# Attention layer with a gated MLP: first half's down projection as Strassen products of tile pairs, and sums divided between VectorE and GpSimd by a table

## The chip, the cores and the metric

The kernel runs on one core of one Trainium2 chip. The metric is the device time of one execution in microseconds (us), the median of several runs; smaller is better. TensorE multiplies 128x128 weights with up to 512 columns into PSUM, VectorE and GpSimd do element-wise work and reductions, ScalarE does activations and copies, and SyncE (SP) issues most of the DMAs. In the profile they are PE, DVE, POOL, ACT and SP.

## The reference, cut to what matters

One layer on 2048 tokens of width 512, in fp32: the normalized input goes through a linear attention of 32 heads of width 16 and, beside it, through a gated MLP with 1376 hidden units; the attention's output is scaled by silu of the MLP's output and added to the input.

```python
x  = A_x
xn = _layernorm(x, axis=-1)
s  = _A_ref(xn, A_wqkv, A_w_phi, A_wo)
g  = _silu(_B_ref(xn, B_W_gate, B_W_up, B_W_down))
return x + s * g
# _A_ref: phi_q, phi_k = [softmax(+q W_phi), softmax(-q W_phi)] per head, the same of k
#         kv = phi_k^T v ;  z = sum of phi_k ;  o = (phi_q kv) / (phi_q z + 1e-6) ;  o @ wo
# _B_ref: gate = xn @ W_gate ;  up = xn @ W_up ;  h = where(gate > 0, gate, 0) * up
#         return h @ W_down
```

## The kernel before, in words

**Numbers.** Each fp32 operand of a product is split into a high and a low part. ScalarE copies the value into the high part, rounded, and a subtraction on another engine leaves the low part. A product of fp32 quality is then three matmuls (low x high, high x low, high x high), `mm3` at L233. So each matrix that enters a product costs one ScalarE copy and one subtraction, and the subtraction is one of the "sums" that this text speaks of.

**Tiles and halves.** Tokens stand in 16 row tiles of 128; a half of the program's MLP work has 8 of them, seen as two blocks of 512 columns (`BT`). The 1376 hidden units stand in NF = 11 tiles of 128; the last, KEPT = 10, has no partner. The blocks of the normalized, transposed input (`XT`) are combined by Strassen's scheme: `GATE_BLOCKS` are seven combinations, for two blocks of tokens against two halves of the width.

**First half's gate and up projection** (`gate_ops`, L845). For hidden tile f, steps `g{f}.0` to `g{f}.6` are seven Strassen products of 6 matmuls each (2 k-tiles x 3), into three PSUM banks (`ga`, `gc`, `gd`) and a fixed bank `seed`. ScalarE copies `ga` out, then VectorE makes five sums and two fused relu-times-up operations, each with at least one operand in PSUM. The results, `h` of two blocks, are split into `hh` pairs.

**First half's down projection** (`down_ops` L888, `down_part` L893, `last_rows` L1082, all through `down_rows`). For chunks of two hidden tiles (`CHUNKS`, the last has three), and each of the 8 row tiles, 3 matmuls per hidden tile accumulate in a bank `py`, with `hh` as the weight and the split down weights `fd` as the moving matrix. Per chunk and row tile one operation folds the bank onto the output `Y0`/`Y1` in SBUF: ScalarE for the first chunk, VectorE for the others. There are 264 such matmuls, 8 ScalarE copies and 32 VectorE folds. The down weights are loaded, ordered and split by `prep_ops` (L413, `fd<-rawd`), and stored to DRAM (`putfe`) for later use beside the gate weights.

**Second half.** The gate (`gate_ops_2`, L1169) uses two banks and hands `seed` to ScalarE three times per tile, so that VectorE has two sums and two fused operations. The down projection takes hidden tiles by pairs: `PAIRED` has five. For a pair, `pair_weight_ops` (L1257) loads two raw tiles of down weights (`WR`), makes four sums of them (`TT`), and splits the matrices `DA`, `DB`, `DC`, `DD`; `pair_hidden_ops` (L1310) makes four sums of the hidden tiles (`S1` to `S4`) and splits seven matrices into `hh` pairs; `pair_down_ops` (L1327) multiplies them, seven Strassen products of 3 matmuls for each of two column halves, in banks `pA`, `pU`, `pD`, each folded by VectorE onto a transposed output `YT0`/`YT1`. The single tile 10 goes by `single_down_ops` (L1229, bank `pE`). At the end `turn_back_ops` (L1367) applies silu, transposes 32x32 blocks on VectorE, and writes the result to DRAM (`YD`), from which it is loaded as rows (`yd`).

**Attention.** 16 key tiles (`key_ops` L670, `kv_ops`) come before the state; 8 queries' worth of pairs (`query_half_ops`, L932) come after it; `QUERIES` says which are turned by halves, through PSUM, and which whole. The output tiles (`out_tile_ops`, L1118) multiply by `wo` (bank `pso`), then multiply with y and add the input: `yd<-pso,yd` on VectorE, `yd<-yd,sx` on GpSimd, in the last row tile on VectorE.

**What sets the order.** Nothing is scheduled by the compiler: `Plan` (L153) holds a closure per operation name, and `Plan.run` calls them in the order of a written table, `ORDER` (L56 to L150), 2075 names before and 2190 after. `InOrder` (L172) keeps that order on each engine. That is why every instruction in the profile has one line, L184 (in the changed kernel L204). A second table, `PLACES` (L43), gives each buffer its place: two-, four- and eight-KB buffers in SBUF (`u2`, `u4`, `u8`) and seven PSUM banks (`ps`). An instruction waits for its operands, and for the last reader of the buffer that it overwrites.

**Which engine sums.** Before, each call of `add` (L222) names its engine. Sums with an operand in PSUM are on VectorE; nearly all sums of two SBUF operands (low parts, Strassen sums of weights and hidden tiles, `yd<-yd,sx`) are on GpSimd.

Of the kernel before, what the change touches and what calls it, by code (L numbers as in the profile page):

```python
# [16 lines left out]
H = 32  # L17
# [12 lines left out]
QUERIES = [(0, 1, 2), (3, 4, 5, 6, 7)]  # L30
BY_VECTOR, IDLE = 4, 8
KEPT = NF - 1
PAIRED = [(2 * p, 2 * p + 1) for p in range(NF // 2)]
WO_WITH = (4, 5, 6, 7)
# [5 lines left out]
0101011010010101001001  # L40

0123456789abcdefghijklmn7kh2a9kng287ldhkg8dgkhgdkh8kdh8kghd10d89a43k2nl7cb1ji08hcg65fe304jh1lbdankjm
9bl53ef07nj2bdf4jhml2b6c1i0kd4bk8em16g5aed213hjc0e4fln5c0h5ci1ebj29gm0iel1348fkb2154jaigdb24f87k36mc  # L43
5l179da304625m9c1he3adjbifnlh7362b8nfljh3a1ig2j6h1lf0knmb2ejn148hf3kigb489fnhag051c78eb50difnagj75lc
h06i275be8gmh5a4f9lcmh63f1ead4kmh17cj94kgfilbd2hnm34i9g0c

0172345689abcd02453869ba5dc802a639bc57d42a576bc8d79c567ab84b56ad827a09b14c9a82c730281c54b9a467b94206
ac2318d52b3017a534c19024c6153ba241ac509c41bac7210a4cb5974c96174ba150689c348190dcb35a2863bc5249387954
86127ad69b

0123456013162504654236541306105302646411441616114646641441116161641646415302615416540412034601245621
4524062451346461425034256250325616162316540624354535415312301353025163240532160434163410653261463152
0635613504664256152601342450210305324612034265316151064125132360650635103665065421340
# [3 lines left out]
ld1 lk0 lcb Fk0 bn1 pw1 bi1 ap1 ld0 bn0 pw0 ap0 T1 kh0 lk1 Fk1 kl0 kh1 kl1 kc0 lk3 Fk3 lq0 hi1 lo1 T0 hi0 lo0 kc1  # L57
Fq1 lk2 Fk2 kh2 ld2 bn2 pw2 Fq0 pk0.0 pk0.1 kl2 pk0.2 kh3 kl3 pk0.3 bi2 qh0 ql0 qh1 ql1 sums0 lv0 pk1.0 pk1.1 pk1.2
pk1.3 vh_0 ld5 st5 td1 vh_1 vl_0 ld3 ep5 bn3 mx0 th1.0 tl1.0 th1.1 ap2 kc2 kc3 lq1 Fq2 pw3 bi3 T2 qh2 ql2 Fq3 pv0.0
lv1 vl_1 pv0.1 ap3 sh0 vh_2 hi2 lo2 T3 qh3 ql3 pw5 bi5 hi3 lo3 vl_2 vh_3 pv1.0 sums1 tl1.1 pv1.1 pv1.2 ld4 st4 ep4  # L60
vl_3 pw4 q1.1 ex0 sm0 td3 ld6 st6 ep6 pw6 sc0 mx1 ap5 pv1.3 vh1 ld7 st7 z0 ep7 pw7 spill0 ph0 bi4 ap4 pl0 sh1 ex1
vl1 td2 td4 pq1.1 q2.0 sps0 bi6 pk2.0 bi7 ap7 sps1 sm1 sc1 z1 pq2.0 pv0.2 pk2.1 pv0.3 vh0 pk2.2 T5 ld8 hi5 st8 T4
sums2 ap6 pv3.0 ep8 lo5 pw8 pv3.1 pv2.0 pv2.1 vl0 hi4 lo4 pv3.2 hS2 slo2 pk2.3 ld9 mx2 T7 T6 hi7 lo7 sh2 ph1 pv3.3
# [12 lines left out]
ql0.0 sums7 P7.6 P3.6 cW6 P4.6 hS7 slo7 lo15 lo14 P1.7 mx13 sh13 cS7 q6.1 pq6.1 sq6.1 fs0 ft0 fs1 ft1 ex13 mx12 sh12
P6.7 rw2 cU7 fa1 fal1 sm13 sc13 z13 sq4.1 ex12 sm12 P3.7 mx14 rd0 fc0 q6.0 kv10 fb0 fbl0 ph13 pl13 pq6.0 P7.7 fc1
sc12 rw4 P5.6 fs2 ft2 fcl0 aw6 z12 cW7 P4.7 P5.7 P2.6 ph12 pl12 sh14 rw3 aw7 sq6.0 P2.7 ex14 ql0.1 vh13 vl13 au6
sm14 au7 vh14 vl14 q8.0 putwc0 pq8.0 sq8.0 mx15 sh15 sc14 ex15 z14 fd1 fdl1 putwd1 fa0 fal0 putwb0 rd1 putwa0 q7.0
sm15 sc15 fe0 fel0 pq7.0 sq7.0 vh15 vl15 q8.1 pq8.1 rw5 kv13 vh12 kz vl12 sq8.1 qt0.0 ph15 pl15 qm0.0 qs0.0 q7.1  # L80
ql2.0 pq7.1 sq7.1 g0.0 z15 putwa1 g0.1 gt0 g0.2 g0.3 fa4 gm0 kv15 ge0 gf0 fb2 fb1 qe0.0 fs3 g0.4 gp0 qa0.0 gs0 fa2
g0.5 fbl1 fc2 fbl2 putwb2 fa3 ph14 kv12 pl14 ql1.0 fd4 fdl4 fal2 putwa2 of_1 g0.6 gn0 g1.1 qt0.1 gg0 qm0.1 fcl1
putwc1 putwd0 g1.0 gt1 sq3.1 kv14 fal3 fcl2 putwc2 ka kb ha0 g1.5 putwa3 ft3 hc0 hd0 zh zl of_2 fd2 g1.2 fdl2 g1.3
fc3 fcl3 hb0 putwc3 g3.0 gt3 qt2.0 gm1 ge1 gf1 g1.4 qs0.1 g1.6 kT g2.0 gp1 gs1 fe1 fel1 gn1 g2.1 fb3 fbl3 ha1 hb1
fal4 gg1 qt1.0 qm1.0 qs1.0 fd3 putwb1 fdl3 gt2 zp0 zc0 gm2 qe0.1 zp1 zc1 qw0.1 fs4 g2.2 putwd2 rw6 g2.5 g2.3 ge2 gf2
ql2.1 g2.4 gp2 kr gs2 ha2 ft4 fb4 putwd4 dn012 qw0.0 g3.1 hc1 qm2.0 qs2.0 kh1_ putwb3 rd3 fe3 fel3 putwa4 qe2.0
qb0.1 g2.6 g3.2 fbl4 gm3 dn010 hd1 rd5 sf1 dy010 sg1 sl1 ge3 g3.3 gf3 gn2 gg2 g3.4 fs5 ft5 putfe1 putfe0 qb0.0 gp3
# [65 lines left out]
class Plan:  # L153
# [8 lines left out]
    def run(self, order):  # L162
        last = {t: name for name in order for t in self.ops[name][1]}
        for name in order:
            fn, tiles = self.ops[name]
            fn()
            for t in tiles:
                if last[t] == name:
                    self.tiles.pop(t, None)
# [19 lines left out]
def layer_kernel(ctx: ExitStack, tc: tile.TileContext, x, wkT, wqT, wv, wo, wf, cst, out):  # L189
# [698 lines left out]
    def down_ops(c):  # L888
        for j in (1, 0):
            for i in range(TPB):  # L890
                down_part(c, j, i)
# [616 lines left out]
```

## Time and profile before

| | before |
|---|---|
| median of 3 runs | 550.25 us (550.11 to 551.11) |
| the profiled execution | 550.4 us |
| its span in the profile | 548.2 us |
| TensorE | 542.0 us busy, 2572 matmuls |
| VectorE | 440.0 us busy, 650 instructions |
| ScalarE | 310.3 us busy, 552 instructions |
| GpSimd | 468.7 us busy, 377 instructions |
| DMA | 132.99 MB, mean 243 GB/s |

The span is the time from the first to the last instruction that the hardware profiler records; the 2.2 us by which the execution is longer lie around it. A row of the view by groups reads: line, engine, operation, out<-in by the program's names, partitions x elements, count, then busy time and the mean of one in ns, then the idle time before them and what ended it. Busy shares are averages over the span; a wait counts only where the engine that waits is the one that sets the end.

### The profile page before, as it was taken

To read this page: it belongs to the slowest core of one execution; us is meant where nothing else is said; L and a number is where in the kernel's file an instruction comes from. 1 tells how busy PE (TensorE), PEld (TensorE's weight loads), DVE (VectorE), ACT (ScalarE), POOL (GpSimd) and SP (SyncE) were. 2 spreads that over 40 slices of the span, in tenths; PEclk is the share of its full clock that TensorE was granted. 3 is DMA by queue.
4 is the path that set the end of the run, shared out by engine and by line. 5 is a ranking of instruction groups with operands and counts; after the bars stand their busy time and mean duration, and the time that the engine had idled before them with its cause. 6 is when DMAs were issued, how large, how long until landed. Compare 5 with 4: busy or idle time off the path is not lost.

```text
span 548.2 us, 8110 instructions
## 1 busy us (share of the span) xinstructions
PE 542.0 (99%) x2572; PEld 454.4 (83%) x2572; DVE 440.0 (80%) x650; ACT 310.3 (57%) x552; POOL 468.7 (86%) x377
## 2 busy tenths in 40 slices
PE   8999999999999999999999999999999999999996
PEld 8888888888888888888888888888888888888885
DVE  5999898878857898998888636877799999984753
ACT  4998787776464457535353345547636555545620
POOL 1999668899999998998978867988989899999965
PEclk9999999999999999999999999999999999999999
DMA  8567737367898796898867899876755859789987
GB/s 305 210 192 239 192 78 192 77 158 211 228 315 273 283 308 213 259 347 291 281 227 275 248 266 375 342 249 215 242 179 180 288 162 266 226 277 293 240 236 265
DMA packets 83034, 132.99 MB, mean 243 GB/s; under 512 B 7344, under 2 KB 38448, under 8 KB 82096
## 3 DMA queue, kind: packets, MB, share of 16 engines
q1 hardware_dynamic: 79392, 119.83, 65.2%
q0 software_dynamic: 3456, 12.58, 12.0%
q8 instruction: 20, 0.33, 0.2%
q14 instruction: 22, 0.18, 0.1%
q10 hardware_dynamic: 144, 0.07, 0.0%
HBM read 70.58 MB, written 53.48 MB: 226 GB/s over the span
## 4 chain that ended last, share of the span: by engine, by line
PE 99%; DVE 0%; issue 0%
PE seed L184 16%; PE py L184 11%; PE pq L184 8%; PE pso L184 8%; PE gc L184 6%; PE gd L184 5%; PE GD L184 5%; PE ga L184 5%; PE GA L184 5%; PE pU L184 4%; PE pa L184 3%; PE pd L184 3%; PE pnum L184 3%; PE pkv L184 3%; PE pD L184 2%; PE pA L184 2%
## 5 line engine op out<-in xcount | busy, mean ns | idle before, releaser
L184 PE MATMUL py<-fd,hh 128*128 128x512 f32 x264 | 63.5, 389 | 0.0
L184 PEld LDWEIGHTS py<-fd,hh 128*128 128x128 f32 x264 | 49.4, 188 | 10.3
L184 POOL TENSOR_TENSOR phl<-ek,phl 128x1024 fp32r<-128x1024 f32 x16 | 40.2, 2514 | 5.2 <-ACT phl L184 5.1
L184 POOL TENSOR_TENSOR ez<-eq,zB 128x1024 f32<-128x1024 f32 x16 | 38.6, 2417 | 4.2 <-ACT eq L184 3.2
L184 PE MATMUL pso<-wo,oh 128*128 128x512 f32 (+1 forms) x136 | 39.8, 376 | 0.0
L184 DVE TENSOR_TENSOR y<-py,y 128x512 f32<-128x512 f32 x32 | 21.7, 683 | 16.2 <-PE py L184 16.1
L184 PE MATMUL ga<-XT,wa 128*128 128x512 f32 x132 | 33.6, 390 | 0.0
L184 PE MATMUL seed<-XT,WB 128*128 128x512 f32 x120 | 30.6, 390 | 0.0
L184 PE MATMUL GA<-XT,WA 128*128 128x512 f32 x120 | 30.6, 390 | 0.0
L184 ACT ACTIVATE eq<-pnum 128x512 f32<-128x512 f32 x32 | 18.6, 594 | 19.8 <-PE pnum L184 19.7
L184 PEld LDWEIGHTS pso<-wo,oh 128*128 128x128 f32 x136 | 25.0, 188 | 4.7
L184 PEld LDWEIGHTS ga<-XT,wa 128*128 128x128 f32 x132 | 24.6, 188 | 5.0
L184 POOL TENSOR_TENSOR pTl<-ez,pTh 128x1024 fp32r<-128x1024 f32 x10 | 24.3, 2432 | 3.4 <-ACT pTh L184 3.0
L184 PEld LDWEIGHTS GA<-XT,WA 128*128 128x128 f32 x120 | 22.3, 188 | 4.5
L184 PEld LDWEIGHTS seed<-XT,WB 128*128 128x128 f32 x120 | 22.2, 188 | 4.5
L184 PE MATMUL pso<-wo,ol 128*128 128x512 f32 (+1 forms) x68 | 25.6, 376 | 0.0
L184 POOL TENSOR_TENSOR ol<-of,oh 128x1024 fp32r<-128x1024 f32 x8 | 20.0, 2494 | 5.3 <-ACT oh L184 5.2
L184 ACT ACTIVATE eq<-eq 128x512 f32<-128x512 f32 x32 | 18.4, 624 | 8.2 <-DVE eq L184 8.2
L184 POOL DMA_DIRECT2D zacc<-ek x16 | 14.4, 899 | 8.2 <-PE seed L184 5.0
L184 POOL TENSOR_TENSOR lr<-lr,mhalf 128x1 f32<-128x1 f32 x16 | 9.4, 590 | 13.8 <-DVE lr L184 13.7
L184 DVE TENSOR_REDUCE sm<-ek 128x64 f32<-128x1024 f32 x16 | 19.4, 1212 | 2.2 <-ACT ek L184 2.0
L184 POOL TENSOR_TENSOR hh<-s,hh 128x512 fp32r<-128x512 f32 x15 | 20.2, 1371 | 0.9 <-DVE YT L184 0.9
(284 smaller groups left out, 1846.3 us busy)
## 6 DMA issues: line engine op xcount, KB each, us to landing
zacc<-ek POOLq DMA_DIRECT2D x16, 512.0 KB, 4.9
XT<-xts SPq DMA_DIRECT2D x7, 1024.0 KB, 8.8
rawg<-wf SPq DMA_DIRECT2D x11, 512.0 KB, 4.8
ws<-wc SPq DMA_DIRECT2D x20, 256.0 KB, 6.3
ws<-wb SPq DMA_DIRECT2D x20, 256.0 KB, 5.5
ws<-wa SPq DMA_DIRECT2D x20, 256.0 KB, 5.0
ws<-fd SPq DMA_DIRECT2D x20, 256.0 KB, 5.5
WA<-ws SPq DMA_DIRECT2D x20, 256.0 KB, 2.9
```

The costliest lines, as they stand in the source:

```text
L184: return self.tc.keep_in_program_order(op(*a, **k))
```

## The change

**What goes.** `CHUNKS`, `gate_ops`' three-bank form, `down_ops`, `down_part`, `down_rows`, `last_rows`, the output tiles `Y0`/`Y1` in rows and their spill, and the split down weights `fd` with their stores.

**What comes.** The first half uses the second half's functions, with a prefix `z = "a"`: the gate in its two-bank form, five pairs (`EARLY`) by seven Strassen products per column half, and tile 10 singly. Its output is transposed (`aYT0`, `aYT1`), turned back, written to DRAM and loaded as rows, so that all row tiles read y from DRAM. The pairs' weights are made for the first half (`D` names). For pairs 0 and 1 (`SPILLED`) the split weights are also stored to DRAM (`pair_weight_store_ops`) and loaded again for the second half, as tiles `EA` to `ED`; for pairs 2 to 4 they are made a second time from the raw weights (`E` names). `QUERIES` has one query fewer in its first list.

**The table.** `add(None, ...)` takes its engine from `either()`: VectorE if the operation's name is in `ON_VECTOR`, GpSimd otherwise. All sums of two SBUF operands are now called so, except those of the last row tile, which are on VectorE in both programs. `ON_VECTOR` has 88 names, several of them with two or four sums. `ORDER` and `PLACES` are written anew.

```diff
-CHUNKS = [(0, 1), (2, 3), (4, 5), (6, 7), (8, 9, 10)]
...
-QUERIES = [(0, 1, 2), (3, 4, 5, 6, 7)]
+QUERIES = [(0, 1), (2, 3, 4, 5, 6, 7)]
+ON_VECTOR = set("""
+vl_0 tl4.0 vl7 vl6 vl9 fs0 fdl0 fdl1 fs3 ft3 Dt0 fcl0 fal0 lDA0 fal1 ow_1 fcl1 fbl1 pl14 fbl2 Du1 fal2 fcl2 fbl3
...
+""".split())
+EARLY = (0, 1, 2, 3, 4)
+SPILLED = (0,1,)
...
+    def either():
+        return nc.vector if plan.now in ON_VECTOR else nc.gpsimd
+
     def add(engine, o, a, b, op=ALU.add):
-        engine.tensor_tensor(o, a, b, op=op)
+        (engine or either()).tensor_tensor(o, a, b, op=op)
...
-            return high, lambda: add(nc.gpsimd, T[h_][1], T[src], f32(T[h_][0]), ALU.subtract)
...
+    def onto_y(name, z, j, dd, p, first):
+        def go():
+            y = turned_out(z, j)[:, :, dd, :]
+            if first:
+                nc.scalar.activation(y, bank(p), AF.Copy)
+            else:
+                add(nc.vector, y, bank(p), y)
+        op(name, go, p, f"{z}YT{j}")
...
+    def hidden_part(z, name, src):
+        t = f"{z}H{name}"
...
+        op(f"{z}HL{name}", lambda: add(None, T[t][1], T[src], f32(T[t][0]), ALU.subtract), src, t)
...
+    def pair_weight_store_ops(p):
+        for i, c in enumerate("ABCD"):
+            w, r = f"D{c}{p}", f"E{c}{p}"
...
+                for s in range(2):
+                    nc.sync.dma_start(dspill[p][2 * i + s], f32(T[w][s]))
...
+                for s in range(2):
+                    nc.sync.dma_start(f32(T[r][s]), dspill[p][2 * i + s])
...
-        op(f"S1{p}", combine(s1, va, vb, ALU.add, nc.gpsimd), s1, va, vb)
+        op(f"{z}S1{p}", combine(s1, va, vb, ALU.add), s1, va, vb)
...
+        for f in range(NF):
+            gate_ops("a", f)
+        single_weight_ops(KEPT)
+        for p, (fa, fb) in enumerate(PAIRED):
+            if p in EARLY:
+                pair_weight_ops("D", p, fa, fb)
+                if p in SPILLED:
+                    pair_weight_store_ops(p)
+                pair_hidden_ops("a", p, fa, fb)
+                pair_down_ops("a", p)
...
+        plain_down_ops("a", "", (KEPT,), "DE", False)
```

The next two pieces show TensorE's row in the middle of the first half, between the gate products of neighbouring hidden tiles; before, `py` takes `hh` as the weight and `fd` as the moving matrix.

```order
L184 MATMUL gc<-XT,wc 128x512 x6
L184 MATMUL py<-fd,hh 128x512 x6
L184 MATMUL seed<-XT,wb 128x512 x6
L184 MATMUL gd<-XT,wd 128x512 x6
L184 MATMUL gc<-XT,wb 128x512 x6
L184 MATMUL py<-fd,hh 128x512 x6
```

After, the products of a pair stand there, three matmuls each, with the pair's weights `DA` to `DD`.

```order
L204 MATMUL gd<-XT,wd 128x512 x6
L204 MATMUL ga<-XT,wa 128x512 x6
L204 MATMUL pA<-hh,DA 128x512 x6
L204 MATMUL ga<-XT,wa 128x512 x6
L204 MATMUL pU<-hh,DC 128x512 x6
L204 MATMUL pA<-hh,DA 128x512 x3
L204 MATMUL pU<-hh,DB 128x512 x3
L204 MATMUL pA<-hh,DB 128x512 x3
```

The gate products of the input `XT` stay; between them groups of 6 `py` products have been replaced by products of the pair.

VectorE in the same part of the first half, before: the sums of the three-bank gate, each reading a bank (`seed`, `gc`, `gd`, `ga`), beside a reduction of a query.

```order
L184 TENSOR_TENSOR m<-seed,t 128x512
L184 TENSOR_TENSOR y<-gc,m 128x512
L184 TENSOR_TENSOR y<-gd,y 128x512
L184 TENSOR_TENSOR m<-gd,m 128x512
L184 SCALAR_TENSOR_TENSOR m<-ga,m 128x512
L184 TENSOR_REDUCE qs<-ez 128x64
L184 TENSOR_TENSOR gc<-gc,m 128x512
```

After: the shorter gate (`gd`, `ga` are banks), then Strassen sums of hidden tiles (`s`, `u`, `v`) and low parts (`hh<-s,hh`), whose operands are all in SBUF, then folds of `pA` and `pU` onto the transposed output.

```order
L204 TENSOR_TENSOR u<-gd,u 128x512
L204 SCALAR_TENSOR_TENSOR u<-ga,u 128x512
L204 TENSOR_REDUCE qs<-eq 128x64
L204 TENSOR_TENSOR s<-s,u 128x512
L204 TENSOR_TENSOR s<-u,s 128x512
L204 TENSOR_TENSOR v<-u,v 128x512
L204 TENSOR_TENSOR hh<-s,hh 128x512 x2
L204 TENSOR_TENSOR YT<-pA,YT 128x16x32
L204 TENSOR_TENSOR YT<-pU,YT 128x16x32 x2
```

Five operations with two SBUF operands now stand in VectorE's row between the gate's last operation and the folds.

GpSimd in the same part, after: it has the other low parts (`hh`) and the gate weights' low parts (`wa`, `wb`, `wc`) and one Strassen sum (`s<-v`).

```order
L204 TENSOR_TENSOR hh<-u,hh 128x512
L204 TENSOR_TENSOR s<-v 128x512
L204 TENSOR_TENSOR hh<-v,hh 128x512
L204 TENSOR_TENSOR hh<-u,hh 128x512
L204 TENSOR_TENSOR wa<-rawg,wa 128x512
L204 TENSOR_TENSOR hh<-v,hh 128x512
L204 TENSOR_TENSOR wb<-tab,wb 128x512
L204 TENSOR_TENSOR hh<-s,hh 128x512
L204 TENSOR_TENSOR wc<-tab,wc 128x512
```

Sums of one pair are thus divided between the two engines, and those of the next gate weights stand between them on GpSimd.

More of the change, by code (lines that the diff above doesn't have):

```diff
@@ L59 @@
[L59 to L63, printed above, removed]
@@ L165, in run @@
             fn, tiles = self.ops[name]
+            self.now = name
             fn()
@@ L319, in a_of @@
         return lambda k: (XT[:, c, 0, k, :], XT[:, c, 1, k, :])
-    def down_rows(p, i, fs, first, last):
-        c = slice(i * P, (i + 1) * P)
-        for m, f in enumerate(fs):
-            (hh, hl), (dh, dl) = f
-            mm(p, hl[:, c], dh, first and m == 0, False)
-            mm(p, hh[:, c], dl, False, False)
-            mm(p, hh[:, c], dh, False, last and m == len(fs) - 1)
     H_OF = [2 * (b < 2) + i for b in range(NB) for i in range(2)]
@@ L459, in prep_ops, with down_parts, high, low @@
         parts(wd, 3, lambda: block(1, 1), lambda: u2((P, 2, 2, P), "wd", F32R), raw, "fdl")
-        parts(fd, None, lambda: T[rd], lambda: d_pair("fd"), rd, "fel")
+        if f != KEPT and f // 2 not in EARLY:
+            down_parts()
+        def down_parts():
+            def high():
+                T[fd] = d_pair("fd")
+                nc.scalar.activation(by_tile(T[fd][0], 4), in_order(T[rd], 4), AF.Copy)
+            def low():
+                add(None, by_tile(T[fd][1], 4), in_order(T[rd], 4), f32(by_tile(T[fd][0], 4)), ALU.subtract)
+            op(f"rd{f}", load_down, rd)
+            op(f"fe{f}", high, rd, fd)
+            op(f"fel{f}", low, rd, fd)
         def store(name, i, pair):
@@ L1303, in corner @@
         def corner():
-            return [(*(by_tile(T[f"DD{p}"][:, s], 2) for s in range(2)), block(1, 1))]
-        parts(f"DA{p}", lambda: d_pair("DA"), r_, column)
-        parts(f"DB{p}", lambda: d_pair("DB"), t_, tables(f"DB{p}", 0))
-        parts(f"DC{p}", lambda: d_pair("DC"), t_, tables(f"DC{p}", 2))
-        parts(f"DD{p}", lambda: u2((P, 2, 256), "DD", F32R), r_, corner)
-    def pair_hidden_ops(p, fa, fb):
-        ua, va, ub, vb = f"U{fa}", f"V{fa}", f"U{fb}", f"V{fb}"
-        s1, s2, s4 = f"s1{p}", f"s2{p}", f"s4{p}"
-        def combine(o, a, b, kind, engine):
+            return [(*(by_tile(T[f"{e}D{p}"][:, s], 2) for s in range(2)), block(1, 1))]
@@ new lines, in pair_weight_ops, with store, load @@
+        parts(f"{e}A{p}", lambda: d_pair("DA"), r_, column)
+        parts(f"{e}B{p}", lambda: d_pair("DB"), t_, tables(f"{e}B{p}", 0))
+        parts(f"{e}C{p}", lambda: d_pair("DC"), t_, tables(f"{e}C{p}", 2))
+        parts(f"{e}D{p}", lambda: u2((P, 2, 256), "DD", F32R), r_, corner)
+    def pair_weight_store_ops(p):
+        for i, c in enumerate("ABCD"):
+            w, r = f"D{c}{p}", f"E{c}{p}"
+            def store(i=i, w=w, c=c):
+                if c == "D":
+                    nc.sync.dma_start(dspill[p][6], f32(flat2(T[w])))
+                    return
+                for s in range(2):
+                    nc.sync.dma_start(dspill[p][2 * i + s], f32(T[w][s]))
+            def load(i=i, r=r, c=c):
+                if c == "D":
+                    T[r] = u2((P, 2, 256), "ED", F32R)
+                    nc.sync.dma_start(f32(flat2(T[r])), dspill[p][6])
+                    return
+                T[r] = d_pair(r[:2])
+                for s in range(2):
+                    nc.sync.dma_start(f32(T[r][s]), dspill[p][2 * i + s])
+            op(f"p{w}", store, w)
+            op(f"r{w}", load, r)
@@ L1324, in pair_hidden_ops, with pair_down_ops @@
+        op(f"{z}S4{p}", combine(s4, ub, s2, ALU.subtract), ub, s2, s4)
         for n, src in (("A11", ua), ("A12", ub), ("A22", vb), ("S1", s1), ("S2", s2), ("S3", va), ("S4", s4)):
-            hidden_part(f"{p}{n}", src, nc.gpsimd)
-    def pair_down_ops(p):
+            hidden_part(z, f"{p}{n}", src)
+    def pair_down_ops(z, p):
+        e = "E" if p in EARLY and not z else "D"
+        begins = z and p == 0
         def stationary(w, i, x):
-            if w == "DD":
-                return [T[f"DD{p}"][:, s, x * P:(x + 1) * P] for s in range(2)]
+            if w == e + "D":
+                return [T[f"{w}{p}"][:, s, x * P:(x + 1) * P] for s in range(2)]
@@ L1419, in register @@
             prep_ops(f)
-            gate_ops(f)
-        for c in range(len(CHUNKS) - 1):
-            down_ops(c)
         for q in range(NP):
@@ L1426, in register @@
             out_ops(q)
-        for j in (1, 0):
-            for i in range(TPB):
-                last_rows(j, i)
-        gate_ops_2(KEPT)
-        single_down_ops(KEPT)
+        for f in range(NF):
[8 more added lines that the diff above has]
+                pair_down_ops("a", p)
+            else:
+                plain_down_ops("a", f"{p}.", (fa, fb), "fe", p == 0)
+        plain_down_ops("a", "", (KEPT,), "DE", False)
+        gate_ops("", KEPT)
+        plain_down_ops("", "", (KEPT,), "DE", True)
         for p, (fa, fb) in enumerate(PAIRED):
@@ L1434, in register @@
                 reload_ops(f)
-                gate_ops_2(f)
-            pair_weight_ops(p, fa, fb)
-            pair_hidden_ops(p, fa, fb)
-            pair_down_ops(p)
-        for j in range(2):
-            turn_back_ops(j)
+                gate_ops("", f)
+            if p not in SPILLED:
+                pair_weight_ops("E" if p in EARLY else "D", p, fa, fb)
+            pair_hidden_ops("", p, fa, fb)
+            pair_down_ops("", p)
+        for z in ("a", ""):
+            for j in range(2):
+                turn_back_ops(z, j)
         for k in range(KD):
```

513 lines of the change are left out of this document (229 added, 284 removed).

## The prediction

> **What bounds the kernel now.** I read the page first: the busy shares, the 40 slices, then the chain that ended last.
>
> ```profile
> span 548.2 us, 8110 instructions
> ...
> PE 542.0 (99%) x2572; PEld 454.4 (83%) x2572; DVE 440.0 (80%) x650; ACT 310.3 (57%) x552; POOL 468.7 (86%) x377
> ...
> PE   8999999999999999999999999999999999999996
> ...
> DVE  5999898878857898998888636877799999984753
> ...
> POOL 1999668899999998998978867988989899999965
> PEclk9999999999999999999999999999999999999999
> ...
> PE 99%; DVE 0%; issue 0%
> ```
>
> TensorE (PE) is busy in every slice but the first and the last, its clock is full throughout, and the chain consists of it. A share of 99% need not mean that nothing waits, so the next view is TensorE's own waits, and beside it two stretches of the busiest part of the second half.
>
> ```profile
> PE seed L184 <- DVE idle L184: 1.5, 1, 1.5
> ...
> 411.00:438.40 27.40, 27.40 (x128) 22.87 (x128) 25.64 (x37) 15.97 (x29) 25.09 (x21) 1.00 0.73 234
> 438.40:465.80 27.40, 27.40 (x134) 23.06 (x133) 26.28 (x38) 14.46 (x26) 25.93 (x21) 1.00 0.75 214
> ```
>
> The only wait listed is the start-up one. In the two stretches (columns: length, then PE, weight load, VectorE, ScalarE, GpSimd, clock, DMA share, GB/s) VectorE is busy 94 and 96%, GpSimd 92 and 95%, and TensorE still never stops. So the time is the sum of TensorE's instructions, and two engines stand close behind it. Whatever shortens TensorE's list shortens the kernel, as long as these two keep up.
>
> **The change part by part: TensorE.** The pace of a 512-column product is read off the end of the program, where such products stand in an unbroken row.
>
> ```profile
> L184 PE MATMUL py<-fd,hh 128*128 128x512 f32 x264 | 63.5, 389 | 0.0
> ...
> 529.77 0.62 PE L184 MATMUL pso<-wo,oh 128*128 128x512 f32 x2
> ...
> 539.97 0.62 PE L184 MATMUL pso<-wo,oh 128*128 128x512 f32 x2
> ```
>
> Between the two starts lie 15 groups of three products, 45 in 10.20 us: 0.2267 us each (389 ns is one product's latency; they overlap). The first half's down projection is the first row: 11 hidden tiles x 8 row tiles x 3 products = 264. Afterwards five pairs need 2 column halves x 7 Strassen products x 3 = 42 each, 210, and the eleventh tile 8 x 3 = 24: 234. Thirty products go: 30 x 0.2267 = 6.8 us. The gate's products keep their number (42 per tile), as do all others. So with everything hidden: 550.4 (the profiled execution; span 548.2, 2.2 around it) - 6.8 = 543.6; the median of the three runs, 550.25, is within 0.2 us of it, so the sums hold for the median too.
>
> **What the cover costs.** The rows that price the other engines:
>
> ```profile
> L184 DVE TENSOR_TENSOR YT<-pU,YT 128x512 f32<-128x512 f32 x30 | 20.2, 681 | 0.5 <-PE pU L184 0.4
> ...
> 440.53 1.28 DVE L184 TENSOR_TENSOR YT<-pD,YT 128x512 f32<-128x512 f32 x2
> 441.73 0.68 DVE L184 TENSOR_TENSOR YT<-pU,YT 128x512 f32<-128x512 f32 x1
> 442.32 0.68 DVE L184 TENSOR_TENSOR U<-GD,U 128x512 f32<-128x512 f32 x1
> ...
> L184 DVE TENSOR_TENSOR eq<-pq,mx 128x1024 f32<-128x1024 f32 x16 | 19.5, 1220 | 0.8
> ...
> L184 DVE TENSOR_TENSOR sums<-pxT,sums 128x256 f32<-128x256 f32 x16 | 6.0, 420 | 0.3
> ...
> 537.19 3.78 POOL L184 TENSOR_TENSOR yd<-yd,sx 128x512 f32<-128x512 f32 x3 [0.16 <-DMA yd<-yd]
> ...
> L184 POOL TENSOR_TENSOR TT<-WR 128x256 f32<-128x256 f32 x10 | 7.5, 801 | 2.7 <-PE py L184 2.7
> ...
> L184 POOL TENSOR_TENSOR ez<-eq,zB 128x1024 f32<-128x1024 f32 x16 | 38.6, 2417 | 4.2 <-ACT eq L184 3.2 <-DMA WA<-ws 0.8 <-DVE YT L184 0.3
> ...
> L184 ACT ACTIVATE V<-seed 128x512 f32<-128x512 f32 x11 | 6.6, 596 | 12.2 <-PE seed L184 12.2
> ```
>
> Back to back VectorE starts one 512-element operation every 0.60 us (three starts in 1.79), 0.08 under its duration; taking 0.08 off the other rows too, 0.34 for 256 elements and 1.14 for 1024. GpSimd: 1.26, 0.75 and 2.41.
>
> VectorE: 28 more folds onto the output than before (120 against 92), 33 fewer gate sums (22 where there were 55), 8 fewer 512-element operations and 6 more of 1024 for transposes: 28 - 33 - 8 = -13 x 0.60 = -7.8, + 6 x 1.14 = 6.8. Then 100 sums of two SBUF operands that GpSimd had or would have had: 64 x 0.60 + 31 x 0.34 + 5 x 1.14 = 54.6. In all 440 + 54 = 494 us, 91% of 541. GpSimd: 34 sums of 512, 10 of 256 and 3 of 1024 fewer, -42.8 - 7.5 - 7.2: 411 us, 76%. ScalarE: 45 more activations at about 0.6, 337 us, 62%; it has the room. The gate of the first half now hands the bank seed to ScalarE three times per tile; the second half did that before (the row V<-seed) with TensorE at 27.40 of 27.40, so nothing for that.
>
> DMA: 14 stores and 14 loads for two pairs' split weights, more raw down weights and rows of y, 16 stores of turned y; against that 20 stores and 11 loads of the old down weights go. SP issues 23 more than 440. What matters is the slack of its weight loads. These are their medians from issue to landing:
>
> ```profile
> WA<-ws SPq DMA_DIRECT2D x20, 256.0 KB, 2.9
> WB<-ws SPq DMA_DIRECT2D x20, 256.0 KB, 3.0
> WC<-ws SPq DMA_DIRECT2D x20, 256.0 KB, 2.8
> WD<-ws SPq DMA_DIRECT2D x10, 256.0 KB, 3.8
> ```
>
> In the old order every weight load stands at least 3.0 us of TensorE's work ahead of the first use of what it brings; in the new one the six closest have 0.45, 0.93, 1.13 (EB and ED, the pair weights read back), 1.81, 1.84 (WA, WC) and 2.49 us (WR). If SP came to each of them only at that point, TensorE would stand still for 2.4 + 2.0 + 1.8 + 1.1 + 1.0 + 0.4 = 8.7 us against a landing of 2.9. But their buffers come free 4.1 to 12 us ahead of the use, and SP may run ahead where nothing earlier in its queue waits. Bounds 0 and 8.7; I take 1, near the end that the old order's rows support. The end (last product, sum, store) keeps its instructions.
>
> So each engine fits on average, and as TensorE waits for neither now, taking sums off GpSimd can gain nothing by itself. The question is the two that now meet: those 100 sums. In the old program VectorE reads at most one SBUF operand beside GpSimd; its two exceptions are in the last 8 us:
>
> ```profile
> L184 DVE TENSOR_TENSOR yd<-pso,yd x3: 424/424/692, 540.7 to 543.5; 128x256 f32<-128x256 f32 x2, 128x512 f32<-128x512 f32 x1
> L184 DVE TENSOR_TENSOR yd<-yd,sx x2: 424/438/453, 542.6 to 544.0; 128x256 f32<-128x256 f32 x2
> ...
> 541.46 1.29 POOL L184 TENSOR_TENSOR yd<-yd,sx 128x512 f32<-128x512 f32 x1 [0.49 <-DVE yd L184]
> 542.58 0.45 DVE L184 TENSOR_TENSOR yd<-yd,sx 128x256 f32<-128x256 f32 x1
> ```
>
> The two yd<-yd,sx are the same instruction. The second ran with GpSimd idle and took 424 ns, just as the form with a PSUM operand does. The first started 0.17 us before a GpSimd sum ended and took 453. It is one sample, but it is the only one of its kind, and it is longer. It fits VectorE being held until GpSimd's reads are over, and also being slowed by a quarter while both run. Nothing in the trace excludes that it is chance.
>
> The Trainium skill ("SBUF — State Buffer", section "Who interferes with whom") has a rule that speaks against the change: a VectorE instruction with two SBUF inputs and a GpSimd instruction that reads SBUF exclude each other, and the second to issue waits until the first is done; one with a single SBUF input does not contend. The 29 ns agree, as far as one sample can; no run so far shows a full exclusion. By that rule the sum comes to the forecast, without it to the first rival.
>
> I price the exclusion where it is densest. From the last gate product of hidden tile 1 (operation g1.6) to the first of tile 7 (g7.0), the order holds 475 products of 512 columns and 48 of 256 (half the pace): 107.7 + 5.4 = 113.1 us of TensorE. In the same stretch GpSimd has 45 sums of 512, 45 of 256, 7 of 1024: 56.7 + 33.8 + 16.9 = 107.4 us. VectorE has 45 two-operand sums (31, 13, 1): 18.6 + 4.4 + 1.1 = 24.1, and some 83 us of others (91 operations at 0.60, 18 at 1.14, small ones 8), 107 in all. Without contention both fit, at 95%, as in the stretches quoted. If the two take turns, GpSimd's and those 45 need 131.5 us where there are 113.1: 18.4 too many. VectorE's side says the same: waiting for half of a GpSimd sum (mean 1.11 us) 95 times in 100 is 0.52 x 45 = 24 us, 131 in all. Bounds: nothing (if 29 ns was chance), 18 here if turns are taken in full. Of the other 57, 20 stand in the 36 us before, where GpSimd by the same counts has a fifth idle, and the rest lie apart: up to 6 more, I take 2. Results finished ahead of their use absorb some of it: I take 4. Turn-taking costs 18 + 2 - 4 = 16 us.
>
> I take full turns as the likeliest, since both readings of the longer sample charge VectorE, which is at 95% there: 550.4 - 6.8 + 1 + 16 = 560.6, for the median 560.5. **Forecast: 560.5 us, its own range 552 to 572.5** (8 of the 16 absorbed and no load late: 551.6; or the full 24 of VectorE's side, 4 of the late loads, and 1 more where the rest lies apart: 572.6).
>
> **The rivals.** *No contention* (0.26): the 29 ns were chance; VectorE and GpSimd run at 95% beside TensorE as in the second half. 550.4 - 6.8 + 1 = 544.6, from 543.5 to 549 by the loads. For it: nothing else in the trace shows the two disturbing each other, and 96% was borne. Against: the one sample. *Slowed, not held* (0.16): each two-operand sum runs about a quarter longer, 45 x 0.14 = 6 us on VectorE's 107, 113 of 113: TensorE loses 1 to 7 us, 545.6 to 551.6, middle 548.5. *VectorE too full without contention* (0.07): from tile 1's gate on it is at 95% for 200 us rather than 55; if folds come late, the PSUM banks that they free are missing and TensorE stops. It decides once VectorE passes 100% in a stretch of some 30 us: 5% over for 150 us is 7.5, 552. Against: the old stretches at 96%. That the 30 products don't go is not possible by the order.
>
> **How the numbers follow.** Forecast 0.51, no contention 0.26, slowed 0.16, VectorE too full 0.07. A measurement here tells 0.2%, 1.1 us, from no change. Faster by more: 0.25 + 0.09 of the slowed + 0.01 of the full = 0.35. Within: 0.01 + 0.04 + 0.01 + 0.01 of the forecast = 0.07. Slower: 0.50 + 0.03 + 0.05 = 0.58. Both signs hold much, and leaving out the rival at 544.6 would leave out more than 2 in 10, so the range goes from 543.5 to 572.5.
>
> **What would show it.** TensorE at 2542 products and a row pA/pU/pE in place of py; if its busy time falls by less than 6 us, the first term is wrong. Turn-taking: two-operand VectorE sums of 512 elements with a mean well over 690 ns (up to 1.3 us), GpSimd sums of 512 over 1.3, TensorE's waits for hh and wa to wd in 130 to 280 us. If these sums show 690 beside a busy GpSimd, contention is refuted and the time should be 543.5 to 549. If they are long and TensorE has no idle all the same, the slack that I put at 4 us was far larger. A late load shows as TensorE waiting for a DMA into EB, ED, WA or WC at 310 to 470 us. If TensorE waits for YT's folds instead, it was VectorE's fill.

## The result, and the profile after

The changed kernel takes 591.3 us (median of 4 runs, 589.85 to 592.1) against 550.68 us before (4 runs beside it): ratio 1.0732, 95% interval 1.0704 to 1.0761. The profiled execution took 590.99 us with a span of 589.2.

The page of the changed kernel, with the rows that were shown of before:

```profile
span 589.2 us, 8142 instructions
...
PE 549.2 (93%) x2542; PEld 449.2 (76%) x2542; DVE 546.9 (93%) x743; ACT 334.6 (57%) x597; POOL 433.8 (74%) x330
...
PE   9999999989897898898989999999999899879996
...
DVE  5999999989999999899999999999999998998955
...
POOL 0888766757687798889789895577859899585552
PEclk9999999989999999899989999999999999999999
...
PE 56%; DVE 27%; DMA 6%; issue 5%; POOL 3%; SPq 2%; ACT 1%; DVEq 0%; POOLq 0%; ACTq 0%
```

The 30 products are gone (2542 for 2572), but TensorE is no longer the whole chain: 27% of it is VectorE, which is busy for 547 us where the count of its instructions gave 494. GpSimd, relieved, is at 74%. TensorE's waits, the four longest (us in all, times, longest):

```profile
PE pA L204 <- DVE YT L204: 4.1, 3, 2.3
PE gd L204 <- DVE v L204: 4.0, 3, 1.5
PE gd L204 <- DVE YT L204: 3.2, 1, 3.2
PE pz L204 <- DVE kvacc L204: 3.2, 1, 3.2
```

All four are waits for VectorE, three of them for a fold or a gate operation, and none in the whole list is for a DMA. So VectorE is the late one, and its groups say with which instructions. First a group with one operand in PSUM, then four of the moved sums, all of 512 elements:

```profile
L204 DVE TENSOR_TENSOR YT<-pA,YT 128x512 f32<-128x512 f32 x58 | 39.3, 682 | 0.5 <-PE pA L204 0.2
...
L204 DVE TENSOR_TENSOR hh<-v,hh 128x512 fp32r<-128x512 f32 x6 | 7.8, 1296 | 0.0
L204 DVE TENSOR_TENSOR s<-v 128x512 f32<-128x512 f32 x5 | 7.3, 1453 | 0.2
L204 DVE TENSOR_TENSOR hh<-s,hh 128x512 fp32r<-128x512 f32 x7 | 7.0, 1005 | 0.0
...
L204 DVE TENSOR_TENSOR wa<-rawg,wa 128x512 fp32r<-128x512 f32 x3 | 5.3, 1780 | 0.0
```

The same operation on the same number of elements takes 682 ns with a PSUM operand and, on average over its group, 1005 to 1780 with two SBUF operands. The timeline of the two engines shows why, for one of the three wa<-rawg,wa (columns: start, length, engine). VectorE first:

```profile
180.23 2.88 DVE L204 TENSOR_TENSOR wa<-rawg,wa 128x512 fp32r<-128x512 f32 x1
183.03 0.68 DVE L204 TENSOR_TENSOR u<-gd,u 128x512 f32<-128x512 f32 x1
```

And GpSimd in the same 3 us:

```profile
180.00 2.56 POOL L204 TENSOR_TENSOR phl<-ek,phl 128x1024 fp32r<-128x1024 f32 x1 [2.47 <-ACT phl L204]
```

GpSimd's sum began 0.23 us earlier and ended at 182.56; VectorE's ended at 183.11, 0.55 us later, which is about its own work. It had stood still for 2.2 us, and the gate operation behind it, u<-gd,u, stood with it.

### The profile page after: what moved, and what is told of

It is laid out like the page before. It is cut to its first block, busy times and chain, and to the rows that moved or that the text cites. A ratio compares the mean times of both kernels' runs of the same rounds, so it can differ in the third digit from the quotient of the medians.

```text
span 589.2 us, 8142 instructions
## 1 busy us (share of the span) xinstructions
PE 549.2 (93%) x2542; PEld 449.2 (76%) x2542; DVE 546.9 (93%) x743; ACT 334.6 (57%) x597; POOL 433.8 (74%) x330
## 4 chain that ended last, share of the span: by engine, by line
PE 56%; DVE 27%; DMA 6%; issue 5%; POOL 3%; SPq 2%; ACT 1%; DVEq 0%; POOLq 0%; ACTq 0%
PE seed L204 12%; PE pq L204 6%; PE gd L204 6%; PE ga L204 5%; PE pA L204 5%; PE pU L204 5%; DVE YT L204 3%; PE pso L204 3%; PE pa L204 3%; DVE hh L204 2%; PE pkv L204 2%; PE pd L204 2%; SPq L204 2%; PE pE L204 2%; PE pv L204 2%
## 5 line engine op out<-in xcount | busy, mean ns | idle before, releaser
L204 POOL TENSOR_TENSOR ez<-eq,zB 128x1024 f32<-128x1024 f32 x15 | 36.6, 2446 | 11.7 <-DVE TX L204 5.0
L204 DVE TENSOR_TENSOR YT<-pA,YT 128x512 f32<-128x512 f32 x58 | 39.3, 682 | 0.5 <-PE pA L204 0.2
L204 DVE TENSOR_TENSOR YT<-pU,YT 128x512 f32<-128x512 f32 x54 | 36.4, 681 | 3.4 <-PE pU L204 3.2
L204 PE MATMUL seed<-XT,wb 128*128 128x512 f32 x144 | 37.1, 393 | 0.0
L204 ACT ACTIVATE hh<-s 128x512 fp32r<-128x512 f32 x30 | 18.5, 626 | 25.5 <-DVE s L204 21.9
L204 PE MATMUL pA<-hh,DA 128*128 128x512 f32 x96 | 28.4, 418 | 4.8 <-ACT hh L204 2.4
L204 PEld LDWEIGHTS seed<-XT,wb 128*128 128x128 f32 x144 | 26.9, 190 | 6.1 <-ACT u L204 0.3
L204 PEld LDWEIGHTS ga<-XT,wa 128*128 128x128 f32 x144 | 26.8, 188 | 5.8 <-ACT zB L204 0.3
L204 PE MATMUL pU<-hh,DC 128*128 128x512 f32 x96 | 28.1, 410 | 2.6 <-ACT pU L204 1.8
L204 PE MATMUL ga<-XT,WA 128*128 128x512 f32 x120 | 30.5, 390 | 0.0
L204 POOL TENSOR_TENSOR hh<-v,hh 128x512 fp32r<-128x512 f32 x16 | 22.9, 1434 | 10.1 <-ACT hh L204 8.1
L204 PEld LDWEIGHTS pA<-hh,DA 128*128 128x128 f32 x96 | 18.9, 201 | 10.3 <-issue 2.5
```

The lines of the kernel that those rows point to most:

```text
L204: return self.tc.keep_in_program_order(op(*a, **k))
```

## The experiments

**What a hold is, by itself.** A program without the layer runs VectorE operations in a row beside GpSimd sums, in sections; in these, `va`, `vb`, `ga`, `gb` are in SBUF and `bank` in PSUM.

```diff
+    def two(o):
+        nc.vector.tensor_tensor(o, va, vb, op=ALU.add)
+    def banked(o):
+        nc.vector.tensor_tensor(o, bank, vb, op=ALU.add)
+    def scaled(o):
+        nc.vector.tensor_scalar(o, vb, one[:, 0:1], one[:, 1:2], op0=ALU.mult, op1=ALU.mult)
+    def reduced(o):
+        nc.vector.tensor_reduce(o, vb.unsqueeze(2), axis=AX.X, op=ALU.add)
+    def pool(o):
+        nc.gpsimd.tensor_tensor(o, ga, gb, op=ALU.add)
```

> No layer at all (its output is a constant): eleven sections, one after the other, of VectorE operations of 512 elements beside or without GpSimd sums of 512. Theory: two SBUF operands take 0.69 us alone; beside GpSimd sums each waits for the running sum to end, so the two engines alternate, 1.9 us a pair; with a PSUM operand 0.69 beside GpSimd; the two-elements-a-cycle form is held too, the one-element reduction is not; beside GpSimd fills, which read nothing, two operands are not held. Rival (slowed, not held): the two-operand sum beside GpSimd 0.8 to 0.95 us with GpSimd at 1.3. Where PSUM forms stand between the two-operand ones, the hold is paid once for each two-operand sum, 0.6 us on average.

The timeline of it, twelve operations to a row: two SBUF operands alone, GpSimd alone, both together, a PSUM operand beside GpSimd, the scaled form alone and beside GpSimd, the one-element reduction beside GpSimd, and two SBUF operands beside GpSimd fills.

```profile
3.54 8.66 DVE L39 TENSOR_TENSOR d<-va,vb 128x512 f32<-128x512 f32 x12
...
12.50 15.98 POOL L39 TENSOR_TENSOR g<-ga,gb 128x512 f32<-128x512 f32 x12
...
28.70 19.62 POOL L39 TENSOR_TENSOR g<-ga,gb 128x512 f32<-128x512 f32 x12
...
28.85 20.02 DVE L39 TENSOR_TENSOR d<-va,vb 128x512 f32<-128x512 f32 x12
...
49.30 8.66 DVE L39 TENSOR_TENSOR d<-bank,vb 128x512 f32<-128x512 f32 x12
...
65.54 6.94 DVE L39 TENSOR_SCALAR d<-vb,one 128x512 f32<-128x512 f32 x12
...
72.92 16.81 DVE L39 TENSOR_SCALAR d<-vb,one 128x512 f32<-128x512 f32 x12
...
99.22 8.61 DVE L39 TENSOR_REDUCE d<-vb 128x512 f32<-128x512 f32 x12
...
115.46 8.66 DVE L39 TENSOR_TENSOR d<-va,vb 128x512 f32<-128x512 f32 x12
```

Together, the two-operand sums need 20.02 us for twelve instead of 8.66, and GpSimd 19.62 instead of 15.98: 1.67 us a pair, a fifth less than the 2.05 that the 1.33 and 0.72 of each alone make one behind the other, so their ends overlap. A PSUM operand, the reduction and GpSimd fills change nothing (8.66, 8.61, 8.66). The theory's turn-taking is shown, the rival "slowed" (0.8 to 0.95 us) is refuted; the pace was put too high, at 1.9. And the scaled form is held too: 16.81 for 6.94. It has one operand and runs at double rate (in the old kernel, below, 547 ns for 512 elements and 804 for 1024 where it wasn't held, 257 ns for the 512 more; a plain sum goes from 0.68 to 1.21 us). That had spoiled the run that is told next, which was made before this one.

The last expectation missed. In the two sections where PSUM forms stand between the two-operand sums, such a sum took 0.91 us with one of them in between and 0.80 with three, after a first one of 1.66: 0.2 and 0.1 us of hold, not 0.6. GpSimd's sums took up to 1.59 there instead of 1.26. In so regular a row the engines fall into step, one round in 1.67 us; how long a hold is depends on where in GpSimd's sum it begins.

**The sums without the hold, first attempt.** In the changed kernel, each sum of the table becomes an operation of one operand in the same place.

```diff
     def add(engine, o, a, b, op=ALU.add):
+        if engine is None and plan.now in ON_VECTOR:
+            nc.vector.tensor_scalar(o, b, mhalf, mhalf, op0=ALU.mult, op1=ALU.mult)
+            return
         (engine or either()).tensor_tensor(o, a, b, op=op)
```

> The changed kernel with the 100 table sums still on VectorE, in the same places, but each as an operation of the same output size that reads one SBUF operand instead of two (the subtraction or addition itself is left out: the second operand times a constant). Theory (VectorE's two-operand sums are held until GpSimd's running operation ends): no operation is held, VectorE's busy time falls from 547 by the 59 us of holds and some 9 us of shorter operations to about 479 us, TensorE's idle goes, 544 to 548 us. Rival (VectorE is too full, by count and not by holds): nearly as many operations stand in front of the folds, 575 to 590 us. Rival (the rest of the change, the order and the reloaded weights, costs by itself): 555 to 570 us with TensorE waiting for something else than VectorE's sums.

Measured: 579.75 us, ratio 1.0539 (1.0514 to 1.0565). That is far from the theory's time and in the range of the rival "VectorE is too full". But the form was wrong for the purpose, as its largest group says:

```profile
L204 DVE TENSOR_SCALAR hh<-hh,mhalf 128x512 fp32r<-128x512 f32 x19 | 18.6, 986 | 1.2 <-ACT hh L204 1.2
```

986 ns where it takes 0.58 us alone (6.94 for 12): it is held as well. By itself this run decides nothing.

**Second attempt, with a form that is not held.**

```diff
+            nc.vector.tensor_reduce(o, b.unsqueeze(len(b.shape)), axis=AX.X, op=ALU.add)
```

> The changed kernel with the 100 table sums as reductions over one element each on VectorE: same places, same output size, one SBUF operand, and no faster rate (the one-operand form of run one_operand ran at two elements a cycle, 547 ns for 512 and 804 for 1024, and was held too). The sums themselves are left out. Theory: none is held, all 512-element ones take 690 to 700 ns, VectorE about 488 us busy, and the time 544 to 550 us. Rival (the new order costs by itself, holds or not): 570 to 585 us, as in one_operand. Rival (one operand is held as well): these operations again above 1000 ns on average.

Measured: 543.5 us (542.79 to 544.07), ratio 0.9876 (0.9862 to 0.9891). Its busy row, the low parts' group on VectorE, and all waits of TensorE:

```profile
PE 535.6 (99%) x2542; PEld 446.8 (82%) x2542; DVE 488.4 (90%) x743; ACT 333.9 (62%) x597; POOL 412.6 (76%) x330
```

```profile
L204 DVE TENSOR_REDUCE hh<-hh 128x512 fp32r<-128x512 f32 x19 | 12.8, 676 | 0.9 <-ACT hh L204 0.7
```

```profile
PE seed L204 <- DVE idle L204: 1.5, 1, 1.5
PE pfold L204 <- DMA wkT<-wkT: 1.2, 1, 1.2
```

With as many operations in the same order on the same engines, of the plain length, TensorE never stops after the start. So the whole 47.8 us between 543.5 and 591.3 come with the holds (some 5 of them through the clock, see the last section). "VectorE too full" and "the new order costs by itself" are refuted: VectorE is at 90%. The holds are 546.9 - 488.4 = 58.5 us on VectorE and 433.8 - 412.6 = 21.2 on GpSimd. Taken one by one, the 100 sums are 121.8 us long in the changed kernel and 62.1 in this run, VectorE's other 643 operations 467 and 468; 60 of the 100 were held by more than 0.05 us, 0.99 on average. A stand-in reads one operand fewer and could have saved a wait for it, but VectorE is idle as long in front of the 100 in both runs, 1.7 and 2.1 us.

**All sums on GpSimd.** The table is emptied (`ON_VECTOR = set()`).

> The changed kernel with an empty table: all 100 sums on GpSimd. Theory: nothing is held, VectorE falls to about 424 us, but GpSimd has 42, 45, 41, 42 and 39 us of sums in five 30 us stretches of TensorE's work in the first half's products and 68 in 60 us later: about 59 + 8 us too many, 600 to 615 us with TensorE waiting for GpSimd. Rival (VectorE too full): VectorE has 24 us less work there, so faster than the changed kernel's 591, 555 to 575 us.

Measured: 634.55 us, ratio 1.1514 (1.1463 to 1.1566).

```profile
PE 569.9 (90%) x2542; PEld 461.9 (73%) x2542; DVE 437.7 (69%) x643; ACT 334.7 (53%) x597; POOL 523.2 (83%) x430
```

```profile
PE pA L199 <- POOL hh L199: 13.1, 10, 3.0
```

GpSimd becomes the late engine, as the theory has it, and a VectorE that is only 69% busy (437.7 us, where 424 were expected) helps nothing. But it is 20 us more than the 615 at which the forecast ended. TensorE's mean granted clock is 0.952 in this run (0.989 in the changed kernel, 0.999 where it never stops): of 570 us busy that is some 27 us, and I had not counted on it. GpSimd also waits 22 us for VectorE's `v` in this run, so the order, which was written for the table, may take part. In this order the table does pay against all sums on GpSimd; it doesn't pay for the work that the first half's pairs add.

**The table alone, in the old kernel.** Its sums of two SBUF operands are called through the same `either()`, with the names that it has; nothing else changes.

```diff
+ON_VECTOR = set("""
+vl_0 tl4.0 vl7 vl6 vl9 fs0 fdl0 fdl1 fs3 ft3 Dt0 fcl0 fal0 lDA0 fal1 ow_1 fcl1 fbl1 pl14 fbl2 Du1 fal2 fcl2 fbl3
...
-            add(nc.gpsimd, tb[:, 0], block(0, 1), block(0, 0), ALU.subtract)
+            add(None, tb[:, 0], block(0, 1), block(0, 0), ALU.subtract)
```

> The old kernel with its own order and products, and only the table's part of the change: those 59 names of the table that it has (71 sums: 36 of 512 elements, 30 of 256, 5 of 1024) go from GpSimd to VectorE. Theory: 0.4 to 0.58 us of hold for each, 28 to 41 us on VectorE, beside 40 us of plain work; where VectorE is over 90% full already (27 of the 71 stand there) TensorE waits: 556 to 566 us. Rival (no contention, or only fill): VectorE at 480 us of 548, 550 to 552 us.

> As before_table, with the 71 sums as one-operand operations of the same size on VectorE (the sums themselves are left out). Theory: no holds, 550 to 552 us. Rival (fill): the same time as before_table.

> As before_table (the old kernel with 71 sums moved to VectorE, 601 us), with those as one-element reductions of one SBUF operand; the sums themselves are left out. If the 28 us of holds measured in before_table make its 50 us: 550 to 556 us. If the place in VectorE's row does (an operation that waits there for ScalarE or a DMA keeps everything behind it waiting): 585 to 600 us, as in before_one_operand, with VectorE's operations at their plain lengths.

Measured: 600.68 us (ratio 1.0898, 1.0856 to 1.094) with the sums, 597.04 (1.0853, 1.083 to 1.0877) with the scaled form, which is held, and 573.91 (1.0434, 1.0417 to 1.0451) with the form that isn't. The busy rows of the first and the last:

```profile
PE 557.2 (93%) x2572; PEld 457.5 (76%) x2572; DVE 504.9 (84%) x721; ACT 310.0 (52%) x552; POOL 398.3 (66%) x306
```

```profile
PE 549.3 (96%) x2572; PEld 453.2 (79%) x2572; DVE 476.1 (83%) x721; ACT 310.1 (54%) x552; POOL 391.4 (68%) x306
```

All three theories missed. With the sums the time is 35 us over the range; the scaled form is as slow as its rival had it, but is held and so tests nothing; and the last lies halfway between its two ranges: 504.9 - 476.1 = 28.8 us of holds make 26.8 us of time, and the other 23.7 us over 550.2 come without any hold, on a VectorE that is 83% busy. The old order was written with those sums on another queue. Put into VectorE's row they can wait there for their operands, with everything behind them: VectorE is idle for 16.3 us in front of the 71, against 1.7 in front of the changed kernel's 100. TensorE's longest wait in the last run, 4.6 us, and VectorE's row ahead of it:

```profile
PE GD L190 <- DVE V L190: 5.6, 2, 4.6
```

```profile
466.01 0.87 DVE L190 TENSOR_REDUCE TT<-TT 128x256 f32<-128x256 f32 x2 [3.80 <-POOL TT L190]
...
474.28 1.22 DVE L190 TENSOR_REDUCE pTl<-pTh 128x1024 fp32r<-128x1024 f32 x1 [1.17 <-ACT pTh L190]
475.42 0.68 DVE L190 TENSOR_TENSOR V<-GD,V 128x512 f32<-128x512 f32 x1
```

Two moved sums stand there: one waits 3.8 us for the table's first half, which is still GpSimd's, the other 1.2 us for ScalarE's high part, and the gate operation that TensorE wants comes after them. This wait is shown; the others I haven't traced. Fullness probably takes part too: between 106.7 and 117.1 us and between 170.3 and 180.4 VectorE is idle for 0.03 us each, and TensorE, which never stopped for these products before, stands still for 1.5 and 1.3 us. So an engine's share of busy time doesn't say whether work can be moved to it without a new order. The changed kernel's order was written for its table, and there this second loss is nil.

**Inside and outside the dense stretch.** The last two runs are the one with 543.5 us, with real two-operand sums only in the stretch that the prediction priced, and only outside.

```diff
-        if engine is None and plan.now in ON_VECTOR:
+        if engine is None and plan.now in ON_VECTOR - TWO:
```

> As one_operand_1x (543.5 us, nothing held), but the 45 table sums of the stretch that the prediction priced are real two-operand sums again; the other 55 stay one-element reductions, their sums left out. Theory: 24 us of holds there, as in the changed kernel's trace (23.6), and nearly all of it reaches TensorE, since VectorE has 5% to spare: 543.5 + 20 to 25 = 563 to 569 us. Rival (the prediction's own size: 4 us and more are absorbed): 553 to 558 us.

> The complement: the 55 table sums outside that stretch are two-operand sums, the 45 inside are one-element reductions. Prediction's term: 2 us, so 545 to 546 us. Theory: 35.6 us of holds as in the changed kernel's trace, of which the 20 sums just ahead of the stretch and the 30 in the second half reach TensorE where VectorE is at 94% and more: 543.5 + 20 to 26 = 563 to 570 us. If inside and outside add up, the two gains over 543.5 make the changed kernel's 47.8; if not, the holds of one part are paid for by the other's slack.

Measured: 569.98 us inside (ratio 1.0351, 1.0322 to 1.0381) and 568.45 outside (1.0345, 1.0315 to 1.0374). Over 543.5 that is 26.5 and 25.0, together 51.5, near the 47.8 of both at once: they add up. The clock differs, 0.985 inside, 0.996 outside and 0.989 in the changed kernel; (1 - clock) x span is 8.5, 2.3 and 6.5 us. The first two have 4.3 more than the third, about the 3.7 by which the parts exceed the whole. Inside is just over what the theory gave (20 to 25), outside where it put it. The prediction had 14 and 2.

How much of a hold reaches TensorE is read from four stretches that lie at the same places of the program, first in the changed kernel, then in the run where nothing is held (columns: stretch, length, then busy PE, weight load, VectorE, ScalarE, GpSimd, clock, DMA share, GB/s):

```profile
105.59:176.34 70.75, 64.65 (x302) 52.99 (x300) 67.02 (x80) 39.56 (x70) 48.59 (x42) 0.98 0.64 175
176.34:315.83 139.49, 121.99 (x525) 96.32 (x526) 135.38 (x179) 80.28 (x158) 116.87 (x96) 0.98 0.69 231
315.83:441.73 125.90, 125.89 (x575) 104.17 (x574) 121.40 (x170) 67.84 (x113) 93.69 (x63) 1.00 0.87 287
441.73:569.01 127.28, 117.94 (x532) 95.44 (x531) 117.70 (x143) 61.27 (x101) 95.38 (x71) 1.00 0.81 238
```

```profile
104.56:166.33 61.77, 61.77 (x302) 51.84 (x301) 55.83 (x82) 40.96 (x73) 47.28 (x42) 1.00 0.73 198
166.33:281.44 115.11, 115.10 (x527) 95.10 (x526) 109.25 (x176) 78.39 (x154) 103.01 (x96) 1.00 0.83 279
281.44:407.16 125.72, 125.71 (x575) 104.30 (x574) 121.11 (x171) 67.73 (x113) 91.73 (x63) 1.00 0.86 290
407.16:522.72 115.56, 115.56 (x532) 96.15 (x531) 99.83 (x143) 61.30 (x101) 92.18 (x71) 1.00 0.88 262
```

VectorE's busy time less that without holds is the hold, the difference of the lengths is the loss. In the dense stretch, with VectorE at 95% without holds (109.25 of 115.11), 26.1 us of hold cost 24.4. Ahead of it, at 90%, 11.2 cost 9.0. In the second half, at 86%, 17.9 cost 11.7. The slow clock is in these losses: 1.7 us of the 9.0 and 3.4 of the 24.4 (last section). In between there are hardly any two-operand sums, and nothing is lost although VectorE is at 96%.

## Why the prediction was wrong in size

- **TensorE's 30 products, -6.8 us: right.** Without holds the time is 6.65 us under that of before (543.5 to 550.15).
- **The counts of the engines: right.** 494, 411 and 337 us were forecast for VectorE, GpSimd and ScalarE; without holds they are 488.4, 412.6 and 333.9. That so full a VectorE does no harm by itself (the rival "too full") holds too.
- **The reloaded weights, 1 us: nothing was late.** No wait of TensorE for a DMA into EB, ED, WA or WC is among its waits.
- **The mechanism: right.** One sample of 453 ns where 424 was plain had been read as VectorE held until GpSimd's reads end. The traces now show it on 60 of the 100 sums, and the rule of the Trainium skill ("SBUF — State Buffer", section "Who interferes with whom") agrees in each of its parts that the sections tried: against sums on GpSimd, not against fills, not with a PSUM operand, not for a reduction, and also for the two-port mode that the page names beside it, if that is what the one operand at double rate ran in. So the prediction's "one with a single SBUF input does not contend" was too wide: at double rate such an operation is held (16.81 us for 6.94).
- **The price in the dense stretch: right in the hold, 10 to 12 us short in the loss.** The prediction worked out 24 us from VectorE's side and 18 from the two engines' sum, took 18, and took 4 off for results that are ready early. Measured: 24 to 26 us of hold, 24.4 to 26.5 of loss. Of this loss 3.4 us in the changed kernel, and some 8.5 in the run with the inside alone, are the slow clock, for which there was no term. The rest is 18 to 21 us, so 5 to 6 us of the hold are absorbed, near the 4; too small was the 18, the lower of the two prices. This split is a subtraction; no run has the holds at a full clock. (The stretch that I counted, 475 and 48 products and 45 sums, runs from about g1.0 to g9.0; the names that the prediction gave to its ends are mistaken.)
- **The step that failed:** "Of the other 57, 20 stand in the 36 us before, where GpSimd by the same counts has a fifth idle, and the rest lie apart: up to 6 more, I take 2." By itself this part costs 25.0 us. (The 57 are the table's 55 and two sums of the last row tile, which are on VectorE in both kernels.) The step took an average share of idle time on GpSimd for a chance of not meeting it, and sums that "lie apart" for sums that cost nothing. A hold needs only one GpSimd sum that runs at that moment, and GpSimd runs three quarters of the time. Had I used the 0.52 us that I had worked out for the dense stretch for each of the 57 as well, that would have been 30 us of hold, and, by the shares that the stretches show (80% for the 20, 65% for the rest), 21 us of loss in place of 2; with VectorE's 24 in place of the 18 as well, the forecast would have been 560.5 + 19 + 6 = 585.5, some 6 under the measured time, about what the slow clock takes. The upper end of the range had even less for this part than the step allowed, 1 us instead of 6.
- **A term that was missing:** TensorE's mean clock is 0.989 instead of 0.999, 1% of its 549 us or 5 us, which some of the stops bring with them (last section). These 5 us are part of the measured losses above, not to be added to them.

## What to carry to other kernels

Before sums are moved from GpSimd to VectorE, count those whose operands both lie in SBUF: here the 64 of 512 elements took 1.30 us on average instead of 0.68, and all 100 brought 58.5 us of holds, and GpSimd lost another 0.2 us for each; a PSUM operand or a form with one SBUF operand at the plain rate avoids it. An engine's average idle time doesn't cover such holds: even with VectorE at 86% two thirds of them reached TensorE, since in an ordered row what is held keeps the folds behind it waiting. To find what a suspected contention costs in all, replace the instruction by one of the same length that can't contend; it gave the whole loss in one run, but only with a substitute that doesn't contend itself; the first one did.

## What the runs showed of the hardware

A short stop of TensorE can cost more than its length. In the changed kernel TensorE ran one product between 236.1 and 238.8 us, and the granted clock in windows of 2 us was (third last column):

```profile
235.37 0.73 PE L204 MATMUL pA<-hh,DA 128*128 128x512 f32 x2 [0.37 <-POOL hh L204]
237.58 0.50 PE L204 MATMUL pU<-hh,DC 128*128 128x512 f32 x1 [1.48 <-ACT pU L204]
238.80 2.48 PE L204 MATMUL pU<-hh,DC 128*128 128x512 f32 x5 [0.72 <-DVE hh L204]
241.08 1.41 PE L204 MATMUL pA<-hh,DA 128*128 128x512 f32 x3
242.33 0.86 PE L204 MATMUL pU<-hh,DB 128*128 128x512 f32 x3
```

```profile
237.00:239.00 2.00, 0.70 (x2) 0.38 (x3) 2.00 (x4) 1.29 (x4) 0.00 (x0) 0.97 0.12 44
239.00:241.00 2.00, 2.00 (x5) 1.61 (x6) 1.65 (x3) 2.00 (x5) 2.00 (x2) 0.50 0.07 14
241.00:243.00 2.00, 2.00 (x7) 1.55 (x6) 1.68 (x3) 0.22 (x1) 2.00 (x3) 0.68 0.72 253
```

It falls to 0.50 for some 3 us: 2 x (0.03 + 0.50 + 0.32) = 1.7 us of clock are lost, and the 11 products from 238.80 on take 4.4 us, where they would take 2.7 at the pace of the old kernel's end. The same happens after stops of 2.8 us at 119.6 and 2.35 us at 301.7, which makes some 5 us in all and most of what the mean of 0.989 lacks; in the run with all sums on GpSimd the mean is 0.952. Not every stop does it: after the two longest, 3.2 us at 189.3 and at 527.2, the clock stays at 1.00, and what tells them apart isn't shown. The old kernel and the run where nothing is held, whose TensorE doesn't stop, have no such stretch ahead of their last product.

GpSimd is held in turn: in the pairs run its sums took 19.62 us for twelve instead of 15.98. And one hold can span several GpSimd sums, one behind the other: in the old kernel with the table, one DC<-TT,DC of 512 elements took 4561 ns while GpSimd ran three sums:

```profile
L190 DVE TENSOR_TENSOR DC<-TT,DC 128x512 fp32r<-128x512 f32 x1 | 4.6, 4561 | 0.0
```

```profile
550.71 2.85 POOL L190 TENSOR_TENSOR hh<-s,hh 128x512 fp32r<-128x512 f32 x2
553.38 1.40 POOL L190 TENSOR_TENSOR hh<-V,hh 128x512 fp32r<-128x512 f32 x1
```
